# Attention projections on row halves of the TensorE array for six head pairs, and a new instruction order, in a float32 kernel of linear attention and a Fourier-mixing MLP

## The chip, the core and the metric

The kernel runs on one core of one Trainium2 chip. Its time is device time in microseconds (us), the median of three runs. The profile is that of one execution, taken by the hardware profiler; its span runs from the first to the last instruction of the core, and the execution's own time is a little longer than its span. TensorE (PE) multiplies matrices and transposes through an identity; its weight loads are a row of their own (PEld). VectorE (DVE), ScalarE (ACT) and GpSimd (POOL) do the elementwise work, SyncE (SP) issues nearly all DMAs.

## The reference

Everything is float32. Eight batches, eight heads, 576 tokens, head dimension 64, 128 random features; the model dimension is 512, the hidden one 2048.

```python
def phi(x):                                   # x = q or k, scaled by D**-0.25
    proj = np.einsum('bhsd,md->bhsm', x, omega)
    sq = np.sum(x * x, axis=-1, keepdims=True) / 2.0
    h = proj - sq
    h = h - np.max(h, axis=-1, keepdims=True)
    return np.exp(h) / np.sqrt(m)
...
kv = np.einsum('bhsm,bhsd->bhmd', k_p, v)
z = np.sum(k_p, axis=2)
num = np.einsum('bhsm,bhmd->bhsd', q_p, kv)
den = np.einsum('bhsm,bhm->bhs', q_p, z)[..., None] + 1e-06
attn = num / den                              # then (B,H,S,D) -> (B,S,H*D) = x
...
X = np.fft.fft(np.fft.fft(x, axis=1), axis=2)
u = x + np.real(X)
un = (u - mean(u)) / np.sqrt(var(u) + 1e-06)
out = u + np.maximum(un @ w_ch1, 0.0) @ w_ch2
```

The term `sq` drops out when the maximum is subtracted, so the kernel computes only `proj`.

## The kernel before

The work has two stages. In the first, the attention runs over 32 head pairs (two heads of one batch, `NP = 4` pairs a batch), three pairs at a time as three streams (`NS = 3`: pairs n, n + 3, n + 6, ... belong to one stream). After the four pairs of a batch comes its Fourier mixing (`mix`), done with matrix products against cosine and sine tables after folding; the sums go to DRAM (`us`). Between these the first 512 rows of the MLP (`plain`, four tiles of 128 rows) are computed in the ordinary way, the two weight matrices are loaded and converted (`weights`, `narrow`), and their sums for the second stage are prepared. The second stage computes the other 4096 rows in eight blocks of 512, with products split by a Strassen-like scheme (`first_of`, line 1239; `product_of`, line 1419).

A pair runs so. SyncE loads k and q (`loads`, two buffers, `NKQ = 2`) and v (`load_v`, three buffers). Of every pair there are 18 chunks of 64 columns and 128 rows; two chunks at a time are turned by TensorE (`transposed`, line 511, nine transposes in three groups, the k chunks first), and ScalarE moves them to `kqT` (line 521). The group that holds q chunks also waits for q; the last group gives the buffer back. The projections follow (`pairs_of`, line 593): for each of the nine 128-column blocks of `kqT`, whose two 64-row halves are two different chunks, four matmuls of a 64x64 tile against `om2` (64x128, twice, in the upper and lower partitions). Each works on one quarter of the array. A float32 matmul appears in the profile as two passes, a transpose as one. VectorE takes the maximum (line 537), ScalarE the exponential (line 554), which gives the features `e`. Then k features times v (line 627, on quarters) give `kv`, the q features are turned (line 511, `qeT`, line 528), and the two meet in lines 674 and 682 on column halves. VectorE or ScalarE divides (lines 691 to 703).

The order of all instructions of the first stage is fixed ahead of time by a planner in the file itself. Every piece of work is a `Step` that yields an engine, an estimated duration, the events it needs, the buffers it takes and gives, and, for TensorE, a tiling mode (`whole`, `quarters`, `halves`); the streams are generators of such steps. At each turn the planner chooses one of the waiting steps; the string `PICKS` has one character for each turn that says which, and on which of two engines where the step allows it. So the string alone fixes the sequence on each engine: the durations are used to place steps that can choose among PSUM banks and buffers. The instructions then stand in that order in each engine's queue, and each waits by semaphores for what it needs. The second stage has no such string and is planned by its durations.

TensorE's program of matmuls and weight loads is read by the core from memory as it runs (queue q8 of the profile's third part), while SyncE's loads run on the same 16 DMA engines.

Of the kernel before, what the change touches and what calls it, by code (L numbers as in the profile page):

```python
# [35 lines left out]
PE, ACT, DVE, POOL, SP, NONE = "pe", "act", "dve", "pool", "sp", "none"  # L36
# [3 lines left out]
class Clock(NamedTuple):  # L40
# [20 lines left out]


PICKS = (
    "40e0f03eafdaegebg3bdbbeefccdcccfce8affgg0hhig8ib2La887efjjgeeejjHhighifdjgijdlhhefTfkkefeifhbdfiefhi"
    "hfjgfkd9elelkjdheefdefQRLbce9h77gh7ijg8cbi877ggk7fihjmngeed87TdecedhIa7g9gg99ieeccdHcdggbhfcgfebbaci"
    "ebccebRfiedaeecf98g7fI7hh1hgg89g6gh8eecg96geaefehceaefg78hh7i9bk79jQ9ghjjf86k6ddkgjdldgiiidhfhcgfhhd"
    "eifjhf6ldinliiIlghgjibmmmILfhflkfljafLLL77lkjmehcomL9pjjjdjOa9hj6a8hhibfegbgij87ddQe9jhljiimidkhgmkj"
    "mjgiiilhkfjThfgiikj9jfmfigieiccb7ki9lll8j0k64c59kik5k86lhh7hge7h6ekie5if9ghccdfihddiifaedleeifM75fce"
    "jkd8bjicj8f8imim9fa3j8iglmn9cjfmiib8kdigce7ikiknmkmbh4cpfdbDqSZllmnFFo5nkaf9bejkllj9ak7hhg9iUhigih8T"
    "lmeIeeggkidlcm7mjdhhddbi77ibKckeiedb4ice8hb6hah8SceghihiMg5eghklfgiih9Ig7gg9b69hh9bKcbgbch54Q78higfi"  # L70
    "deeffg5ddfjcTcdigjeiedfgjhdmInmTjcgfedjhdbh67egkOa9khgkSa9hh5eghdf99bhgdegdacjgckeccgckhfhckdk9jJjij"
    "JQec9agba8cLa75i5ggih6hdUdG6j8jjTPjgg9gk57f5hdieleigIdejeihdiijkiGgibeL7875g7jgh6U8a99mmijh8jfk8kgea"
    "jf9di4gf6c5gei5ea9becjeeecghghbcjcdkfhgglfljkjh9giiackibhe5nebkkf9kJ55o4mkllQmifebek4jij557iikk9jjji"
    "mikhjkkhkiikikjlinij5JnPfjNF7efdffcc78b5kjj8lk6bae6i95W98jg3fhRefm66nfikkehhkmlcccffifhihjj6nldmiimn"
    "lmldofkhndamm48a47j4hf5khaaa8nkmm68mkj76lijknSk8iiJi9gknihne43lmccicjomaEONU76jh7mopkhjbinpijbhkkiIl"
    "5bh7jidl6klbSfihhagll50jT7eg7eikhjhh7gkhfikj0gcdcifdbiehijfmlcn2Ob5mm3k9acdc8h9g5h7eedhdgd77cbQd5gg2"
    "e9e367e78hibbMG4bbb58ccK9dLa8cfea2fecKdebecdeccefbIPbcb9hdhM6k52gbbMg5bfP7NR987ac98NPb85e8de5e6c5ec9"
    "ahagabc9dcecaeee5d8ababb9c899cKd9bedccde7fc98dgSghedggig18789bi6G45jjUi1e9gRc5863f4feL69afg3MRd8b4Eg"
    "gdc6bbe4ddeehdheimfhbifamfgccebcddhidjgjedddeT47466g4PgQ4eff1a977bb3bb833aLJ579b395I99ab9e998dbab694"
    "7c9dddgdf5hhhPfe9ead9cce7G9ed34438ge9FdHc9dcLd5ed98LcddbhheabedabddfhePdcfaafffI4daaJ9Mcce8beefd4cc2"  # L80
    "adeab27OOOM8a9K5659b0664dccdda7a2ccMccd40296cdeIP97ce8bcf6c8ddabac1aaI9d52bb9e661abec5D915G7bcd5Ed9C"
    "5bHHa9983763a3b4399F5414335aaaaE499954423225530320210"
)


# [195 lines left out]
def kernel(  # L281
# [12 lines left out]
    B, H, S, D = q.shape  # L294
# [13 lines left out]
    P = 128  # L308
# [4 lines left out]
    NV = 3  # L313
    NKQ = 2
    NE = 7


    TP = 128
# [31 lines left out]
    buffers = dict(  # L350
        kq=NKQ, turned=NS, e=NE, e1=NS, kv=NS, x0=1, x1=1, fold=1, half=1, y=1,
        bmp=2, sign=1, slab=4, u=2, unT=1, ht=NFC, ur=1, **{f"vd{i}": 1 for i in range(NV)},
# [7 lines left out]
    def got():  # L360

        return listing.got, psum_of(listing.got)
# [16 lines left out]

    def load_v(n):  # L380
        b, pr = divmod(n, NP)
        yield Step(SP, 0.63, 4.0, take=(f"vd{n % NV}",), makes=("vd", n), kb=500, bias=0.52)
        nc.sync.dma_start(
            vds[n % NV][:, :, 0:D],
            v[b, 2 * pr : 2 * pr + 2].rearrange("i (p r) d -> (i p) r d", r=R),
        )

    def loads_v():
        for n in range(B * NP):
            yield from load_v(n)  # L390
# [139 lines left out]
    def softmax(n, ts, num, b, es):  # L530

        yield Step(DVE, 0.063 + 0.267 * num, bias=-0.56)
        nmx = small.tile([P, 2, 4], F32, name="nmx", tag="nmx", bufs=4)
        pps = psum_of(b)
        nc.vector.tensor_reduce(  # L537
            nmx[:, :, 0:num],
            pps[:, :, 0 : MF * num].rearrange("p b (c m) -> p b c m", m=MF),
            axis=AX.X,  # L540
            op=ALU.max,
            negate=True,
        )
        size = "e" if num == 4 else "e1"
        for i, one in enumerate(b):
            if num == 4 or not i:
                yield Step(
                    ACT, 1.0 if num == 4 else 0.5, 0.04, take=(size,),
                    give=(one,) if num == 4 else (b,), makes=("e", n, ts[i]), bias=0.31,
                )  # L550
                e = att.tile([P, 4 if num == 4 else 2, MF], F32, name="e", tag=size, bufs=NE if num == 4 else NS)
                es[ts[i]] = e
            for c in range(num):
                nc.scalar.activation(  # L554
                    out=e[:, c + (i if num == 1 else 0), :],
                    in_=pps[:, i, MF * c : MF * c + MF],
                    func=AF.Exp,
                    bias=nmx[:, i, c : c + 1],
                )

    def attn(n):
# [13 lines left out]
        )  # L575
        es = {}

        def pairs_of(js, *ts):


            yield Step(
                PE,
                0.23 * len(js),
                mode="quarters",
                after=(("kqT", n, js[-1] // 4 * 4), "om2"),
                take=("duo",),
                give=("turned",) if js[-1] == R - 1 else (),
            )
            b, pps = got()
            for m, j in enumerate(js):  # L590
                for c, i in ((0, 0), (1, 1), (0, 1), (1, 0)):
                    rows, cols = slice(D * c, D * c + D), slice(D * i, D * i + D)
                    nc.tensor.matmul(  # L593
                        pps[cols, c, MF * m : MF * m + MF],
                        lhsT=kqT[rows, j, cols],
                        rhs=om2[rows, :],
                    )
            yield Fork(softmax(n, ts, len(js), b, es))


        yield from pairs_of(range(0, 4), 0, 1)
        yield from pairs_of(range(4, 5), 2)
        yield from pairs_of(range(5, R), 3, 4)

        def place(c):
# [4 lines left out]
        def feature(c):  # L610
# [7 lines left out]
            mode="quarters",  # L618
            after=tuple(("e", n, t) for t in range(3)) + (("vd", n),),
            take=("duo",),  # L620
# [3 lines left out]
        for r in range(R):  # L624
            for i, h in ((0, 0), (1, 1), (0, 1), (1, 0)):
                rows, cols = slice(D * i, D * i + D), slice(D * h, D * h + D)
# [9 lines left out]
        def keep():  # L636
# [24 lines left out]
            mode="halves",  # L661
            after=(("kv", n), ("qeT", n, 0), ("qeT", n, 1), ("qeT", n, 5)),
            take=("duo",),
# [526 lines left out]
    def pairs(start):  # L1190
        for n in range(start, B * NP, NS):
            yield from attn(n)
# [364 lines left out]
```

## Time and profile before

| what | value |
|---|---|
| median of 3 runs | 1185.65 us (1182.2 to 1187.07) |
| profiled execution: its own time | 1187.5 us |
| its span | 1185.6 us, 31878 instructions |
| TensorE busy | 1165.1 us (98%), 12765 passes |
| weight loads | 1044.6 us (88%) |
| VectorE, ScalarE, GpSimd busy | 697.8, 470.1, 417.6 us |
| first stage, to the first line-1239 product | 428.44 us |
| TensorE, ScalarE, VectorE busy in it | 412.77, 300.22, 315.95 us |
| mean granted clock | 0.996 |

The share of the span of the chain that ended last is 92% TensorE. TensorE's busy time includes ends that are modelled, so the price of a group of instructions is read from its start to the start of the next group, less the idle time that the timeline puts before that next group. In a timeline line the columns are the start and length in us, the engine and line, the operation, what is written from what, the tile of the array (rows*columns), the shape, the number of passes, and in brackets the idle time before the group and what ended it.

### The profile page before, as it was taken

What the parts mean: (1) busy time and instruction counts of PE and PEld (TensorE: products, weight loads), DVE (VectorE), ACT (ScalarE), POOL (GpSimd) and SP (SyncE); (2) the same over time, 40 slices, a digit from 0 to 9 for tenths busy, and PEclk for the clock granted to TensorE, in tenths of its full rate; (3) what the DMA queues carried; (4) which work ended last, traced back from release to release, by engine and by line L of the source; (5) the groups of instructions that cost most, each with busy time, mean ns of one, the idle gap of its engine ahead of it and who ended that gap; (6) DMA issues with size and microseconds to landing.
All of it is one profiled execution on the core that took longest, in us unless ns stands there. A gap on an engine that the chain in (4) does not pass through costs nothing.

```text
span 1185.6 us, 31878 instructions
## 1 busy us (share of the span) xinstructions
PE 1165.1 (98%) x12765; PEld 1044.6 (88%) x12765; DVE 697.8 (59%) x1488; ACT 470.1 (40%) x1597; POOL 417.6 (35%) x496
## 2 busy tenths in 40 slices
PE   7999999999999999999999999999999999999998
PEld 6888888779877868998998998999999899899898
DVE  4898899886656542762572582473374276266255
ACT  5988888868654212222222222222222222222211
POOL 2353544444344314314304314323422431431421
PEclk8999999999999999999999999999999999999999
DMA  8566856656654161761682482384195085177155
GB/s 250 165 186 182 252 172 194 186 164 193 188 194 157 45 212 50 261 211 63 205 264 74 154 290 100 99 294 149 48 303 192 10 290 191 54 240 240 63 165 192
DMA packets 144708, 205.71 MB, mean 174 GB/s; under 512 B 49072, under 2 KB 58544, under 8 KB 144560
## 3 DMA queue, kind: packets, MB, share of 16 engines
q1 hardware_dynamic: 144064, 203.41, 54.1%
q8 instruction: 101, 1.65, 0.6%
q14 instruction: 47, 0.39, 0.1%
q10 hardware_dynamic: 496, 0.26, 0.1%
HBM read 171.90 MB, written 35.91 MB: 175 GB/s over the span
## 4 chain that ended last, share of the span: by engine, by line
PE 92%; ACT 2%; DVE 2%; DMA 2%; issue 1%; SPq 1%; POOL 0%; DVEq 0%; ACTq 0%
PE banks L1239 33%; PE banks L1419 30%; PE banks L1055 5%; PE banks L1032 5%; PE banks L511 5%; PE banks L593 4%; PE banks L627 3%; PE banks L674 2%; PE banks L972 2%; PE banks L836 1%; ACT e L554 1%; PE banks L786 1%; PE banks L796 1%; DMA kq<-in_q_dram 1%; PE banks L847 1%
## 5 line engine op out<-in xcount | busy, mean ns | idle before, releaser
L1225 DVE CUSTOM_DVE_ANT_0 hid<-banks,s 128x256 f32<-128x256 f32 x192 | 79.6, 422 | 255.4 <-PE banks L1239 250.5
L1419 PE MATMUL banks<-wl,sums 128*128 128x128 f32 x1792 | 217.5, 275 | 0.0
L1419 PEld LDWEIGHTS banks<-wl,sums 128*128 128x128 f32 x1792 | 208.9, 192 | 0.5
L1253 ACT ACTIVATE s<-banks 128x256 f32<-128x256 f32 x192 | 73.6, 383 | 261.7 <-PE banks L1239 261.7
L554 ACT ACTIVATE e<-banks,nmx 128x128 f32<-128x128 f32 x576 | 164.7, 437 | 16.3 <-DVE nmx L537 15.7
L1239 PE MATMUL banks<-unT,w 128*128 128x256 f32 x704 | 167.5, 379 | 0.0
L1239 PEld LDWEIGHTS banks<-unT,w 128*128 128x128 f32 x704 | 132.7, 190 | 17.9 <-issue 0.5
L1394 ACT ACTIVATE s<-banks 128x128 f32<-128x128 f32 x168 | 46.5, 277 | 242.6 <-PE banks L1419 196.0
L1239 PE MATMUL banks<-tt,w1s 128*128 128x256 f32 x512 | 126.2, 379 | 0.0
L1306 POOL TENSOR_TENSOR hs<-hid 128x256 f32<-128x256 f32 x64 | 46.4, 725 | 202.9 <-DVE hid L1225 178.6
L537 DVE TENSOR_REDUCE nmx<-banks 128x8 f32<-128x1024 f32 (+1 forms) x96 | 89.0, 952 | 34.1 <-PE banks L593 31.8
L1239 PEld LDWEIGHTS banks<-tt,w1s 128*128 128x128 f32 x512 | 97.2, 190 | 13.3
L1399 DVE TENSOR_TENSOR part<-banks,s 128x128 f32<-128x128 f32 x168 | 48.8, 291 | 89.0 <-PE banks L1419 88.7
L1419 PE MATMUL banks<-wl,hid 128*128 128x128 f32 x768 | 97.6, 275 | 0.0
L1419 PEld LDWEIGHTS banks<-wl,hid 128*128 128x128 f32 x768 | 93.5, 192 | 1.2
L1306 POOL TENSOR_TENSOR hs<-hid,hs 128x256 f32<-128x256 f32 x64 | 46.5, 727 | 120.4 <-issue 95.4
L593 PE MATMUL banks<-om,kqT 64*64 64x128 f32 x2304 | 78.4, 276 | 2.4 <-issue 0.9
L1239 PE MATMUL banks<-unT,w1s 128*128 128x256 f32 x320 | 80.7, 379 | 0.0
L966 POOL TENSOR_TENSOR rstd<-rstd,mhalf 128x1 f32<-128x1 f32 x36 | 24.1, 668 | 146.1 <-DVE rstd L964 145.1
L1419 PE MATMUL banks<-wl,hs 128*128 128x128 f32 x576 | 74.9, 275 | 0.4 <-DVE part L1399 0.4
L593 PEld LDWEIGHTS banks<-om,kqT 64*64 64x64 f32 x2304 | 63.9, 134 | 12.2 <-issue 4.3
L1419 PEld LDWEIGHTS banks<-wl,hs 128*128 128x128 f32 x576 | 70.0, 192 | 0.9 <-DVE part L1399 0.6
(129 smaller groups left out, 1957.0 us busy)
## 6 DMA issues: line engine op xcount, KB each, us to landing
wl<-w2l SPq DMA_DIRECT2D x392, 256.0 KB, 3.6
raw<-in_moe_w_ch_dram SPq DMA_DIRECT2D x32, 512.0 KB, 5.2
kq<-in_k_dram SPq DMA_DIRECT2D x32, 288.0 KB, 4.5
kq<-in_q_dram SPq DMA_DIRECT2D x32, 288.0 KB, 5.1
vd<-in_v_dram SPq DMA_DIRECT2D x32, 288.0 KB, 4.6
u<-us SPq DMA_DIRECT2D x36, 256.0 KB, 4.0
ur<-us SPq DMA_DIRECT2D x36, 256.0 KB, 3.8
out_dram<-ur SPq DMA_DIRECT2D x34, 256.0 KB, 2.4
```

The lines of the kernel that those rows point to most:

```text
L511: nc.tensor.transpose(ps[:, (j - j0) * 128 : (j - j0 + 1) * 128], src(j), ident[:])
L537: nc.vector.tensor_reduce(nmx[:, :, 0:num], pps[:, :, 0 : MF * num].rearrange("p b (c m) -> p b c m", m=MF), axis=AX.X, op=ALU.max, negate ...
L554: nc.scalar.activation(out=e[:, c + (i if num == 1 else 0), :], in_=pps[:, i, MF * c : MF * c + MF], func=AF.Exp, bias=nmx[:, i, c : c + 1],)
L593: nc.tensor.matmul(pps[cols, c, MF * m : MF * m + MF], lhsT=kqT[rows, j, cols], rhs=om2[rows, :],)
L1032: nc.tensor.matmul(hp[:, 0:TP], lhsT=w1[:, dc, 128 * fc : 128 * fc + 128], rhs=unTs[key][:, dc, :], start=(dc == 0), stop=(dc == NDC - 1),)
L1055: nc.tensor.matmul(yp[:, 0:DM], lhsT=hs[fc][:, 128 * i : 128 * i + 128], rhs=w2[:, fc, :], start=(fc == 0), stop=(fc == NFC - 1),)
L1225: nc.vector._custom_dve(TENSOR_ADD_SAT, out=o, in0=ps, in1=sb, s0=FMAX, s1=0.0)
L1239: nc.tensor.matmul(ps[:, 0:HT], lhsT=left(dc), rhs=right(dc), start=start and dc == 0, stop=(dc == D2 - 1), skip_group_check=True,)
L1253: nc.scalar.activation(out=s[:], in_=ps[:, 0:HT], func=AF.Copy)
L1306: nc.gpsimd.tensor_tensor(out=o, in0=l, in1=r, op=op)
L1399: nc.vector.tensor_tensor(out=part[:, t, 128 * m : 128 * m + 128], in0=ps[:, 0:128], in1=saved[with_][:], op=ALU.add,)
L1419: nc.tensor.matmul(ps[:, 0:128], lhsT=left[:, f], rhs=wls[j, i, n][:, f], start=start and f == 0, stop=(f == 3), skip_group_check=True,)
```

## The change

It has three parts. For the first six pairs (`n < NWIDE`), `pairs_of` issues two matmuls a block in place of four: each takes a 64x128 tile of `kqT` on one half of the array's rows, and writes all 128 output partitions. The planner's step gets a tiling mode `rows` and a duration of 0.25 a block in place of 0.23. All other pairs keep the quarters. The planner's duration for issuing a v load goes from 0.63 to 1.15. And `PICKS` is replaced: the first characters are alike, most of the rest differs, so the order of the first stage changes on every engine. The work itself is otherwise the same.

```diff
 PICKS = (
-    "40e0f03eafdaegebg3bdbbeefccdcccfce8affgg0hhig8ib2La887efjjgeeejjHhighifdjgijdlhhefTfkkefeifhbdfiefhi"
...
+    "40e0f03eafdaegebg3bdcbeefccdcccfc8aggh0gjihij8c2M99887eejgffjgHeefgikedlekddkidfffffkkheeeegjiigOKdh"
...
+    NWIDE = 6
...
-        yield Step(SP, 0.63, 4.0, take=(f"vd{n % NV}",), makes=("vd", n), kb=500, bias=0.52)
+        yield Step(SP, 1.15, 4.0, take=(f"vd{n % NV}",), makes=("vd", n), kb=500, bias=0.52)
...
+        wide = n < NWIDE
+
         def pairs_of(js, *ts):
-
             yield Step(
                 PE,
-                0.23 * len(js),
-                mode="quarters",
+                (0.25 if wide else 0.23) * len(js),
+                mode="rows" if wide else "quarters",
                 after=(("kqT", n, js[-1] // 4 * 4), "om2"),
                 take=("duo",),
                 give=("turned",) if js[-1] == R - 1 else (),
             )
             b, pps = got()
             for m, j in enumerate(js):
-                for c, i in ((0, 0), (1, 1), (0, 1), (1, 0)):
-                    rows, cols = slice(D * c, D * c + D), slice(D * i, D * i + D)
+                for c, i in ((0, 0), (1, 0)) if wide else ((0, 0), (1, 1), (0, 1), (1, 0)):
+                    rows, cols = slice(D * c, D * c + D), slice(D * i, P if wide else D * i + D)
                     nc.tensor.matmul(
                         pps[cols, c, MF * m : MF * m + MF],
                         lhsT=kqT[rows, j, cols],
                         rhs=om2[rows, :],
                     )
```

The order on SyncE at the start, which the prediction speaks of, by what is loaded (numbers are issues since the first; w is a piece of a weight matrix, one comma-separated entry is one step):

```
issue   before                                      after
1-14    k q v v k q k w q w k q cs cs               the same
15-20   sn sn w v w v                               w sn sn w v k
21-26   v k cd cd q k                               cd cd v w q k
27-33   w w w q k sd sd                             w v w q sd sd v
```

On TensorE the two orders run as follows after the first pair's k v product (lines of before; passes in brackets):

```
before: 511 k(4) 593(40) 511 e(9) 511 k(5) 627(72) 674(32) 682(8) 511 e(1) 593(32) ...
after:  593(4) 511 e(1) 593(16) 511 k(8) 511 e(8) 511 k(1) 627(72) 674(32) 682(8) 593(16) ...
```

More of the change, by code (lines that the diff above doesn't have):

```diff
@@ L63 @@
 PICKS = (
-    "40e0f03eafdaegebg3bdbbeefccdcccfce8affgg0hhig8ib2La887efjjgeeejjHhighifdjgijdlhhefTfkkefeifhbdfiefhi"
[L65 to L82, printed above, removed]
+    "40e0f03eafdaegebg3bdcbeefccdcccfc8aggh0gjihij8c2M99887eejgffjgHeefgikedlekddkidfffffkkheeeegjiigOKdh"
+    "ddfdgel8dlglkjfhdfefgQeQgLd7787eihfigegbbb88i8f7jhikigjmfdddfdifeiihHdcccffeddccddIHcggafbgaddadbhbf"
@@ new lines @@
+    "cdebRfiddiaeecf877gbe7ii1ihhae7hige7k8hgdfcehghfcGefga8hg7ghhabk89jQ9ghjjf86k6ddkgjdldhigidhcigfIegg"
+    "cdifjhf6kijchljmjblhjjobnHLknjkhkQmgdkjakLMLm87kjjcfed9nbkia9kkif6jaj8iedhheckgj8b7dSckle7eichgjjckl"
+    "miikffhgjjkfefiTflkkiglhghmhjec7b99jjk0jh64d66k9hk97mkhhhhhMef7ehig69dchdg6iaedleldkbcgdbmfmh57bhikg"
+    "g5jg8djibj7a7imim8f3kbjhlmn7dgcm8lknig7fkfmmc6mnollbjipi6ofecbDoecWhlijlghmnlmeccXljnbiohjibikilgnLm"
+    "kiFp6Fgdfjk8i7l9cebb9kahiaagHk7Rfeia46abjedbRfhgaehfa8NKeed5a5f9cceijfhhahccgg6aidgg4SHf98hh47bhigfi"
@@ new lines @@
+    "eeeffe5ehddehfhadiePffdlhfkTjU9hgeihcdfi889cg9h9fhkkiefihSbahh5bghgcbgfhhafhfebajmiefggkgcj9gjiiJJPb"
+    "b9fdbac86j65kjhkk7h78eUj87Uk96kklkfTQkfg9hl6H5jeoipefffghhGfkeeihOjhig8n78l5fam8Wfbb8nllVcha5ghmfj9l"
+    "jmdb6j4hc6ad5hejhbd9deffPediffgghedjkicliiiijkhjhkad9iglbge5ngbkkf9kJ644olkoQifebek4ji6ii57iil9jjjhi"
+    "lklhnkjlhkkjkilinijcYn59FmeLMgddijcc78maldj58cb7ja5Wa9jkhTfkjf3e8mPd6liilgkjdcmjffgnf7dfflmlghkknjkn"
+    "efghPojEkimjfeYanl4nnmf566m44nnjSe9b68l6ljkjljbkkdUihihkb3h5ilfilTdh6ckj6l6le5iemHLIT5j48jbGibkjjj7h"
@@ new lines @@
+    "jahihf4jhflkkamjj9jjm40llbifgkiijahjiifjj0hhjjee5cdjdidfihejT7c37kkk4id98abghah6if7ccecOfcd8db6ii2a9"
+    "gbdfcdfaae53af78ccG7d8Kb9M78cfaggg8RcdgcdgbbK2gcNbacdfNcbfgO642577M9fa9Pdd8bbfdMa9de5OLN5ee75cbbf6aa"
+    "5becbbdeada9fbcd9bfbb5bgaehaQccddg9dabgb8db7kk2LI143gfg556a87f4f46bfQgegcfecQ8fa4eccMRefSf69dfeg7aLE"
+    "9d7ffec6fe3fdchhgiccbQ4daij6ck8ad8jdgegfhc98eh9dgeagbfE6e6d5144b544994c96689ab4466a8485c79e7779e5a89"
+    "6ece65fd5defP8ff33e7cbh7bJIEE9b4gaaga8I3d898Hfe8OcLN49cd9b6N8f88efdeFN9bahghfghe7IebOgeehbac92feLe2c"
@@ L83 @@
+    "dce979ccK9aKJ9b879a0Bd1a54babbb1b4278aKaa7c9Nc9c7aac8c9f6M076198cM65604a87abac83Fbac7499bbG1063b7aKa"
+    "Jc9768971bHC628bcc6b5a6c3647C877550777662230242132110"
 )
```

## The prediction

> **What bounds the kernel now.** I read the windows first: they split the span where the second half of the MLP begins.
>
> ```profile
> core 0: us, PE busy (x) PEld busy (x) DVE busy (x) ACT busy (x) POOL busy (x), PEclk, DMA share, GB/s
> 0.00:428.44 428.44, 412.77 (x7726) 341.58 (x7727) 315.95 (x686) 300.22 (x1090) 179.26 (x187) 0.99 0.60 179
> 428.44:1185.60 757.16, 752.31 (x5041) 703.00 (x5039) 381.81 (x802) 169.85 (x507) 238.29 (x309) 1.00 0.52 170
> ```
>
> From 428.44 us on, TensorE's instruction order is the same in both kernels (the first difference, counted from the end, lies before the line-1239 products), so those 757.16 us stay. What can change lies in the first 428.44 us, and TensorE is the bound there too: it is idle for only 428.44 - 412.77 = 15.67 us. TensorE's waits say what those are.
>
> ```profile
> engine line waited for: us in total, times, longest us
> PE banks L674 <- issue: 4.6, 1, 4.6
> PE banks L511 <- DMA kq<-in_q_dram: 2.0, 2, 1.6
> PE banks L511 <- ACT e L554: 1.9, 2, 1.3
> PE banks L511 <- DMA kq<-in_k_dram: 1.5, 1, 1.5
> PE banks L593 <- issue: 0.9, 1, 0.9
> ```
>
> "Issue" means that nothing the profile shows was waited for. The timeline of TensorE shows where:
>
> ```profile
> 14.22 0.65 PE L593 MATMUL banks<-om,kqT 64*64 64x128 f32 x10
> 15.78 1.10 PE L593 MATMUL banks<-om,kqT 64*64 64x128 f32 x30 [0.91 <-issue]
> 16.81 1.20 PE L511 MATMUL banks<-ident,e 128*128 128x128 f32 x9
> 17.85 0.71 PE L511 MATMUL banks<-ident,kq 128*128 128x128 f32 x5
> 18.49 1.28 PE L627 MATMUL banks<-vd,e 64*64 64x65 f32 x72
> 19.70 0.56 PE L674 MATMUL banks<-kv,qeT 128*64 128x65 f32 x11
> 24.84 1.36 PE L674 MATMUL banks<-kv,qeT 128*64 128x65 f32 x21 [4.57 <-issue]
> ```
>
> Both waits cut a group of equal matmuls in two. Between them lie 30 + 9 + 5 + 72 + 11 = 127 passes, each with its weight load: 254 instructions, [...]. Before the first wait lie 221 passes. So the program's text came late, while the loads had the DMA engines (third column from the end is the clock, then the DMA share):
>
> ```profile
> 20.00:22.00 2.00, 0.26 (x9) 0.13 (x6) 0.40 (x2) 2.00 (x8) 1.46 (x2) 1.00 1.17 319
> 22.00:24.00 2.00, 0.00 (x0) 0.00 (x0) 0.00 (x0) 0.20 (x1) 1.33 (x1) 0.76 1.23 265
> 24.00:26.00 2.00, 1.16 (x23) 1.16 (x24) 0.00 (x0) 0.00 (x0) 0.00 (x0) 0.50 0.63 119
> 26.00:28.00 2.00, 2.00 (x33) 1.65 (x33) 1.19 (x3) 0.89 (x3) 0.00 (x0) 0.50 0.89 255
> ```
>
> The reader sees the clock fall to 0.50 after the wait, and ScalarE run dry as well, so the lost time is not made up elsewhere.
>
> [...] TensorE's instruction queue moved 101 packets, 1.65 MB. [...]
>
> **The change part by part.** Prices come from TensorE's timeline, start to next start:
>
> ```profile
> 43.47 1.10 PE L593 MATMUL banks<-om,kqT 64*64 64x128 f32 x32
> 44.50 0.77 PE L511 MATMUL banks<-ident,e 128*128 128x128 f32 x5
> ...
> 46.07 1.32 PE L593 MATMUL banks<-om,kqT 64*64 64x128 f32 x40
> 47.33 0.33 PE L511 MATMUL banks<-ident,kq 128*128 128x128 f32 x1
> ...
> 63.42 0.81 PE L796 MATMUL banks<-cs_sb,fold 64*128 64x320 f32 x4
> 64.17 1.09 PE L511 MATMUL banks<-ident,e 128*128 128x128 f32 x8
> ```
>
> Four chunks of projections take 1.03 us to the next kind, five take 1.26: 0.23 us a chunk on quarters and 0.11 us for the change of tiling mode (a fit over all groups of the stage gives 0.232 and 0.107).
>
> 1. *Row halves.* 6 pairs x 9 chunks = 54 chunks go from 4 matmuls to 2, so from 8 passes to 4. The only row of this kind is L796: four passes of 320 columns in 0.75 us, less one mode change 0.64, so 0.32 for two side by side. A whole-array pass takes 0.115 us at 128 columns and 0.147 at 160, so near 0.28 at 320: the two do overlap, at 0.04 over a pass. A chunk is two such couples of 128 columns: from 2 x 0.115 = 0.23 to 2 x 0.155 = 0.31. I take 0.25: 54 x 0.02 = +1.0 us (bounds 0 and +4.3).
>
> 2. *Text.* 54 x 8 = 432 instructions go, 1.7 blocks. Priced by the fit, the blocks that start at passes 94, 221, 348 and 475 hold 3.9, 4.3, 5.9 and 3.0 us of TensorE work before; in the changed order they hold 5.2, 5.9, 4.6 and 5.3, and the next one 7.6. Before, the second block came 3.9 + 0.91 = 4.8 us after the first began, which 5.2 covers: -0.91. The third came 24.84 - 15.78 = 9.1 us after; if that stays, 9.1 - 5.9 = 3.2 us of 4.57 remain. I expect less: the same first fourteen DMAs are issued, but the two v loads that kept SyncE's queue busy for 3.45 us from 18.45 no longer come back to back; k, a table and one v load stand there. I take 1.0 left (bounds 0 and 3.2). Later blocks ran through in as little as 3.5 and 3.9 us without a wait before, so the usual fetch is that fast.
>
> 3. *Clock.* From 24.84 to 29.78 us TensorE did work worth 2.70 us by the fit (21 + 8 + 1 + 32 + 4 passes and three mode changes), in 4.94: 2.24 lost. [...]: -2.24.
>
> 4. *Order of the k and q loads.* Two buffers hold k and q, so a pair's load starts when the transposes of the pair two before are done. In TensorE work between them, pair 16's q half has 6.4 us before and waited 1.60 us at 124.75; in the new order it has 8.8. Pair 25 has 4.95 and waited 0.40 at 222.15; now 5.7. Both waits should go: -2.0. Pairs 10 and 13 keep 6.5 and 5.8, as the ones that did not wait for DMA. SyncE's sequence there is nearly the same, so nothing new stands before these loads. The first k wait (1.54 us at 9.03) follows the same DMAs and stays.
>
> 5. *Other reordering.* The new TensorE order has 253 mode changes in this stage against 232: 21 x 0.107 = +2.25 us. 1.7 us of the extra TensorE work of parts 1 and 5 lies before the eighth pair ends, where TensorE waits for ScalarE now (0.57 + 0.19 + 0.42 + 0.35 + 0.16 = 1.69 us between 36 and 60). ScalarE is 99% busy at 40 to 60 us, so it can hide some: I take -0.5. Without that cover, 0. The 1.29 us wait at 89.38 for ScalarE keeps its neighbours in the order: 0. The changed price of the v load (1.15 for 0.63) is no instruction; it acts through the order alone. At the stage's end the last norm transposes stand before 8 matmuls of L1055 (16 passes x 0.43 = 6.9 us) instead of before 12 + 16 passes of other work; two evictions and four adds of line 1100 (2.5 us) have to fit, and do: 0.
>
> Sum: -0.91 - 4.57 + 1.0 - 2.24 - 2.0 + 1.0 + 2.25 - 0.5 = -5.97 us. The profiled execution took 1187.5 us (span 1185.6 and 1.9 around it), so 1181.5 in its terms; it stood 1.85 above the median of 1185.65, which becomes 1179.7. ScalarE is late next: with the gap gone it runs through from 10 to 60 us.
>
> **The rivals.** *Given back.* The text comes half as late and the new order waits for ScalarE or a load in new places, for 3 to 4 us: the 4.3 us of small waits now are spread over many engines, and a searched order shifts all of them. The gain is 2 to 3 us, 1183. For it: the orders on VectorE, ScalarE and GpSimd all differ from the start; against: the pairs finish at nearly the same amounts of TensorE work (0.5 to 3 us apart through most of the stage). *Fetch stays slow.* A k load, a table and more weights now follow without a pause where SyncE before issued nothing from 26.4 to 32.85 us. If each of four blocks takes 9.1 us to come, the waits are 9.1 less 5.9, 4.6, 5.3 and 7.6: 13.0 us, and two clock drops of 2.2 more. Then -7.7 - 2.0 + 3.25 + 17.4 = +10.9: 1196.6, slower. It decides from about 7.4 us a fetch, where the first three waits eat the rest of the gain (3 x 7.4 - 15.8 = 6.4). For it: the one fetch seen in the burst took 9.1; against: at 38 to 48 us, DMA share 0.76 to 0.98, none was late. *Row halves in series.* Four passes of 0.115 are 0.46 a chunk: 54 x 0.21 = 11.3 more than I take, 1191; L796 speaks against it. *More.* The small waits for ScalarE go too, and the fetch is never late: 1.0 + 4.3 us more, 1174.5.
>
> **How the numbers follow.** 0.5% (5.9 us) is about what a measurement of this kernel can tell from no change. The forecast, 4 to 9 us off, has 0.52, and 0.28 of that is past 5.9; "more" 0.12; "given back" 0.20; slow fetch 0.11, serial halves and the like 0.05, of which 0.01 stays inside 0.5%. Faster 0.28 + 0.12 = 0.40; same 0.24 + 0.20 + 0.01 = 0.45; slower 0.15. Range 1174 to 1191: it holds the forecast, "given back" and nearly all of "more" and leaves out the slow fetch. The likeliest case's own range is 1176 to 1182.
>
> **What would show it.** Right: no issue wait over 2 us before 60 us, clock 1.00 in the windows from 22 to 30; projections of 0.25 us a chunk in a 64*128 tile; no wait for q near 120 or 220 us; the first line-1239 product near 422.5 us, and 757 us after it. Wrong: a wait cutting a group in two at every 127th pass, a clock of 0.50 elsewhere, or L554 and L521 in front of TensorE's idle time where they are not now.

## The result, and the profile after

| | before | after |
|---|---|---|
| median | 1186.66 us (20 runs, 1182.20 to 1191.15) | 1182.66 us (20 runs, 1180.12 to 1185.49) |
| profiled execution, its span | 1187.5, 1185.6 us | 1183.56, 1181.8 us |

The ratio of the times is 0.9967, with a 95% interval of 0.9956 to 0.9978: 4.0 us less, 0.33%. That is inside the 0.5% that the prediction took for no change, but twenty runs of each tell it from none. The profiled executions differ by 3.9 us, so they can stand for the medians. In the code after, most of the lines spoken of stand one or two lower (593 is 595, 511 is 512, 627 is 629, 674 is 676, 912 is 914, 1239 is 1241).

The windows of the changed kernel, split at its first line-1241 product (busy us of each engine, then clock, DMA share, GB/s):

```profile
0.00:424.44 424.44, 413.60 (x7510) 340.52 (x7511) 316.61 (x681) 298.72 (x1088) 186.49 (x194) 1.00 0.62 183
424.44:1181.80 757.36, 752.26 (x5041) 703.09 (x5039) 381.93 (x802) 169.85 (x507) 238.26 (x309) 1.00 0.52 169
```

Before, that product began at 428.28 us (the prediction's split, 428.44, lies 0.16 behind its start), so that the second stage took 757.32 us and takes 757.36 now. All of the change is in the first stage, 3.84 us. TensorE is idle for 424.44 - 413.60 = 10.84 us of it, 15.67 before, and 0.8 us busier. The new `PICKS` also moves work between engines: over the whole execution VectorE has five instructions fewer, ScalarE two, and GpSimd seven more (503 for 496). TensorE's waits, by what ended them:

```profile
engine line waited for: us in total, times, longest us
PE banks L512 <- DMA kq<-in_q_dram: 2.8, 2, 2.5
PE banks L512 <- DMA kq<-in_k_dram: 2.2, 1, 2.2
...
PE banks L595 <- issue: 0.8, 1, 0.8
PE banks L676 <- issue: 0.4, 2, 0.2
```

The 4.6 and 0.9 us of "issue" have become 1.2 in three pieces, but the waits for loads of k and q, 3.5 us before, are now 5.0. TensorE's timeline of the place where the 4.57 us stood:

```profile
24.67 0.82 PE L595 MATMUL banks<-om,kqT 64*128 64x128 f32 x9
26.26 0.71 PE L595 MATMUL banks<-om,kqT 64*128 64x128 f32 x7 [0.78 <-issue]
26.90 0.77 PE L512 MATMUL banks<-ident,kq 128*128 128x128 f32 x5
27.60 1.16 PE L595 MATMUL banks<-om,kqT 64*128 64x128 f32 x16
28.69 1.28 PE L629 MATMUL banks<-vd,e 64*64 64x65 f32 x72
29.90 0.49 PE L595 MATMUL banks<-om,kqT 64*128 64x128 f32 x4
30.46 0.91 PE L676 MATMUL banks<-kv,qeT 128*64 128x65 f32 x23
31.59 0.51 PE L676 MATMUL banks<-kv,qeT 128*64 128x65 f32 x9 [0.22 <-issue]
```

Projections stand in a 64*128 tile, 16 passes for four blocks. A group is again cut in two by a wait for nothing that the profile shows, and from one cut to the next lie 7 + 5 + 16 + 72 + 4 + 23 = 127 passes, as before, but holding more work. The instruction queue of the two pages' third part, before and then after (packets, MB, share of the 16 DMA engines' span):

```profile
q8 instruction: 101, 1.65, 0.6%
```
```profile
q8 instruction: 99, 1.62, 0.6%
```

TensorE's 12765 passes with their weight loads are 253 instructions for each of the 101 packets, and 12549 are 254 for each of the 99: the length from one cut to the next, and 432 instructions less are 2 packets less. So a packet is read here as one block of TensorE's text, and such a wait as a block that came late; no view shows when a single packet landed. The windows there:

```profile
22.00:24.00 2.00, 2.00 (x25) 1.67 (x21) 1.97 (x4) 1.59 (x8) 0.51 (x1) 1.00 1.22 291
24.00:26.00 2.00, 1.49 (x17) 1.16 (x14) 1.35 (x4) 2.00 (x8) 2.00 (x2) 1.00 1.16 225
26.00:28.00 2.00, 1.74 (x18) 1.45 (x19) 0.92 (x1) 1.34 (x7) 0.72 (x1) 1.00 0.98 290
```

The DMA share is as high as before (1.16 and 1.22), but the clock stays at 1.00 where it was 0.76 and 0.50. By the same group of 30 passes of L595 (55.39 us; 59.80 before) the changed kernel is 4.4 us ahead; from there to the second stage it loses 0.57. TensorE's timeline shows a place of the loss:

```profile
85.03 0.63 PE L512 MATMUL banks<-ident,kq 128*128 128x128 f32 x4 [2.54 <-DMA kq<-in_q_dram]
```

It waits 2.54 us for the tenth pair's q, which the kernel before did not. SyncE's waits (total, times, longest) and then its timeline lead to what stood ahead of that load:

```profile
SPq L914 <- POOL x L900: 38.0, 6, 15.9
```
```profile
71.97 1.22 SPq L914 DMA_DIRECT2D us<-x  x2
73.30 0.53 SPq L376 DMA_DIRECT2D kq<-in_k_dram  x1
73.92 1.98 SPq L469 DMA_DIRECT2D raw<-in_moe_w_ch_dram  x1
75.99 1.94 SPq L384 DMA_DIRECT2D vd<-in_v_dram  x2
77.98 2.26 SPq L379 DMA_DIRECT2D kq<-in_q_dram  x1
```

Before, the tenth pair's k, the store and q stood so:

```profile
68.80 0.33 SPq L375 DMA_DIRECT2D kq<-in_k_dram  x1
...
77.08 1.90 SPq L912 DMA_DIRECT2D us<-x  x2
...
79.71 0.71 SPq L378 DMA_DIRECT2D kq<-in_q_dram  x1
```

At 71.97 us SyncE comes out of a wait of 15.9 us for GpSimd's `x` (line 900), which a store of the first mixing result needs. Behind it in the queue stand the tenth pair's k, a weight piece, two v loads, and only then q, issued at 77.98. Before, the store stood between k and q. With the 4.4 us that the changed kernel is ahead, 79.71 would be 75.3; its q is 2.7 us later than that. The store itself comes 5.1 us earlier than before. What is new is how much was put behind it: from the store to q pass 6.0 us, where it was 2.6.

### The profile page after: what moved, and what is told of

It reads as the page before. It is cut to its first block, busy times and chain, and to the rows that moved or that the text cites. A ratio compares the mean times of both kernels' runs of the same rounds, so it can differ in the third digit from the quotient of the medians.

```text
span 1181.8 us, 31441 instructions
## 1 busy us (share of the span) xinstructions
PE 1165.9 (99%) x12549; PEld 1043.6 (88%) x12549; DVE 698.5 (59%) x1483; ACT 468.6 (40%) x1595; POOL 424.7 (36%) x503
## 4 chain that ended last, share of the span: by engine, by line
PE 90%; ACT 4%; DVE 2%; DMA 2%; issue 1%; POOL 0%; SPq 0%; DVEq 0%; POOLq 0%; ACTq 0%
PE banks L1241 33%; PE banks L1421 30%; PE banks L1057 5%; PE banks L1034 5%; PE banks L512 4%; PE banks L595 3%; ACT e L555 3%; PE banks L676 2%; PE banks L629 2%; PE banks L974 2%; PE banks L838 1%; PE banks L788 1%; DMA kq<-in_q_dram 1%; PE banks L798 1%; ACT kqT L522 1%
## 5 line engine op out<-in xcount | busy, mean ns | idle before, releaser
L595 PE MATMUL banks<-om,kqT 64*64 64x128 f32 (+1 forms) x2088 | 79.8, 275 | 2.2 <-ACT kv L645 0.8
L595 PEld LDWEIGHTS banks<-om,kqT 64*64 64x64 f32 (+1 forms) x2088 | 64.6, 138 | 13.3 <-issue 6.6
```

The lines of the kernel that those rows point to most:

```text
L595: nc.tensor.matmul(pps[cols, c, MF * m : MF * m + MF], lhsT=kqT[rows, j, cols], rhs=om2[rows, :],)
```

## The experiments

Eleven runs: nine new kernels, one of them twice, and the changed kernel again. `PICKS` is adapted in each new kernel so that only what is named differs: where loads move, SyncE's order; where row halves come or go, the projections on TensorE. The planner's choice of PSUM banks is fixed in all of them, apart from the repeat of the changed kernel, to that of the kernel they start from, which adds lines to the file (595 is 607, 629 is 641, 676 is 688, 914 is 926).

| kernel | median us | ratio to before, 95% interval | runs |
|---|---|---|---|
| quarters in the new order | 1188.37 | 1.0013 (1.0002 to 1.0025) | 22 |
| row halves in the old order | 1189.48 | 1.0024 (1.0012 to 1.0035) | 22 |
| row halves for three pairs, old order | 1187.00 | 1.0002 (0.9988 to 1.0017) | 14 |
| new load order at the start, else before | 1187.90 | 1.0006 (0.9995 to 1.0018) | 14 |
| before, tables late | 1186.23 | 0.9993 (0.9976 to 1.0009) | 14 |
| after, tables late | 1183.26 | 0.9969 (0.9958 to 0.9981) | 22 |
| after, tenth pair's loads ahead of the store | 1182.30 | 0.9968 (0.9957 to 0.9979) | 22 |
| after, second pair's k and q first | 1181.32 | 0.9953 (0.9939 to 0.9967) | 22 |
| the same again | 1181.98 | 0.9956 (0.9939 to 0.9972) | 13 |
| after, both moves | 1180.55 | 0.9946 (0.9927 to 0.9966) | 8 |
| after, again | 1182.06 | 0.9960 (0.9943 to 0.9976) | 11 |

### One part of the change at a time

The new order with the projections on quarters:

```diff
-    NWIDE = 6
+    NWIDE = 0
```

> The changed kernel with the quarters back for the first six pairs (36 matmuls a pair in place of 18), every engine's order otherwise as in the changed kernel. Theory text: the row halves matter because they thin the program. With quarters the first fetched blocks hold 3.7, 4.5, 6.0, 2.8 us of TensorE work in place of 5.2, 5.9, 4.6, 5.3, so an issue wait of 2.5 to 4.5 us comes back between 18 and 28 us, with the clock at 0.50 after it: +4 to +6 us on the changed kernel, near 1187. Theory order: the new order of loads had removed the wait; then no issue wait over 1 us, and 1 us less than the changed kernel for cheaper projections, 1181.5.

And the old order, old durations, with row halves for the first six pairs (the diff of `pairs_of` alone):

> The kernel before with row halves for the first six pairs and nothing else changed, its own order on every engine. Theory text: the blocks hold 5.1, 5.6, 5.0, 5.2 us instead of 3.9, 4.3, 5.9, 3.0; the issue waits fall from 5.5 us to 1 to 3.5, the clock stays at 1.00, row halves cost 1 us: 1181 to 1184. Theory order: waits as before, 1187.5.

Neither part gains alone: both are slower than before, by 0.13% and 0.24%. In the first the waits for text are back, in the order that had 1.2 us of them, as its timeline shows:

```profile
15.80 1.09 PE L607 MATMUL banks<-om,kqT 64*64 64x128 f32 x27 [0.87 <-issue]
23.75 1.45 PE L688 MATMUL banks<-kv,qeT 128*64 128x65 f32 x21 [2.53 <-issue]
35.66 0.51 PE L688 MATMUL banks<-kv,qeT 128*64 128x65 f32 x9 [1.02 <-issue]
41.59 0.45 PE L641 MATMUL banks<-vd,e 64*64 64x65 f32 x12 [0.91 <-issue]
```

That is 5.3 us in the first 60 (5.5 before, there in two waits), and the clock fell too: 0.50 from 24 to 26 and 0.83 from 26 to 28 us. The second stage begins at 430.06 us, 5.6 after that of the changed kernel. So the row halves, not the order, take these waits away.

In the second kernel the front is as good as hoped (one wait for text of 0.94, clock 1.00, the group that stood at 58.12 before at 54.15), and the 4 us are lost again later: its second stage begins at 430.96, 2.7 later than before. The largest loss, in its timeline (line 696 is 682 of before) and its windows:

```profile
135.88 0.33 PE L696 MATMUL banks<-kv,qeT 128*64 128x65 f32 x2 [2.59 <-issue]
```
```profile
122.00:132.00 10.00, 9.83 (x296) 8.49 (x289) 9.36 (x15) 9.83 (x39) 7.02 (x6) 1.00 0.90 295
132.00:134.00 2.00, 1.29 (x38) 1.15 (x38) 1.61 (x3) 2.00 (x10) 0.74 (x1) 1.00 0.52 179
134.00:136.00 2.00, 0.12 (x2) 0.12 (x2) 0.00 (x0) 0.87 (x4) 0.78 (x1) 1.00 0.69 144
136.00:138.00 2.00, 2.00 (x11) 1.62 (x11) 1.50 (x4) 0.00 (x0) 0.00 (x0) 0.63 0.92 294
138.00:140.00 2.00, 2.00 (x73) 1.98 (x72) 1.86 (x4) 1.87 (x7) 0.00 (x0) 0.51 0.43 96
```

It is the pattern of 24 us over again, with a DMA share of 0.90 over the ten us ahead, a block of text late, and the clock at 0.63 and 0.51 after it, where the kernel before ran through. Two waits for q of 1.46 and 1.19 us at 120.56 and 154.09 come with it. Every block border after the first six pairs has moved against the loads.

To see whether the borders do it, the old order got row halves for three pairs only, so that the borders move half as far:

```diff
-    NWIDE = 6
+    NWIDE = 3
```

> The kernel before, its own order, with row halves for the first three pairs only. The first blocks hold 5.1, 5.6, 4.1, 5.0 us, so the early issue waits are 1 to 2.5 us in sum and the clock stays up. The text is 108 passes shorter than before, not 216, so all later block borders lie elsewhere. Theory borders: the 2.59 us issue wait that row halves for six pairs brought at 136 us (and the clock drop after it) is a matter of where a border falls against a burst; here it is under 1 us: 1183 to 1186. Theory pace: with the front faster, the later loads and text are late anyway; an issue wait of 2 us or more comes near 135 us again: 1188 to 1190.

At 135.50 us there is 0.27 left of the 2.59, but 1.89 stand at 189.60 in its place and 2.17 for a q at 222.39. Its waits for ScalarE grew most, by 3.8 us over before in the first stage. The time, 1187.00, is that of before and lies in neither of the ranges expected. That the place of the wait moves with the borders is seen; which border will meet a burst could not be told ahead.

### The order of the loads, and what they do to the text

The kernel before, with SyncE's first steps in the changed kernel's sequence (w is a piece of a weight matrix, cs, sn, cd, sd are the tables of two issues each, numbers are pairs):

```diff
 k0 q0 v0 v1 k1 q1 k2 w q2 w k3 q3 cs
-sn w v2 w v3 v4 k4 cd q4 k5 w w w q5 k6 sd v5 v6 q6
+w sn w v2 k4 cd v3 w q4 k5 w v4 w q5 sd v5 k6 w v6 q6
```

> The kernel before with only SyncE's issues 13 to 36 put in the sequence that the changed kernel has (the two v loads apart, a weight load and k ahead of them). Theory order: the second block's fetch takes 7.2 us as in the changed kernel, not 9.1, so the wait of 4.57 falls to about 2.7 and the clock drop mostly goes: 1182 to 1184. Theory text: the fetch is as late as before, 4 to 5 us of wait and the clock drop stay: 1186 to 1188.

The wait at 24.52 us is 4.28, and the clock 0.84 and 0.50 from 24 to 28. The order of these loads alone did nothing for the text, and the prediction's thought that a k load and a table in place of two v loads would speed up the fetch has no support.

The opposite test takes loads out of the burst: the four tables (0.90 MB) are loaded only after the sixth pair's q, in each of the two kernels. In the kernel before:

```diff
-cs sn w v2 w v3 v4 k4 cd q4 k5 w w w q5 k6 sd
+w v2 w v3 v4 k4 q4 k5 w w w q5 cs sn cd k6 sd
```

> The kernel before with the four cosine and sine tables (0.83 MB, of which 0.64 were asked for at 12 to 15 us) loaded after the sixth pair's q instead; nothing but SyncE's order differs, quarters throughout. Theory contention: the text comes late because it shares the DMA engines with the burst of loads; 0.64 MB at about 0.29 MB a us is 2.2 us less in front of it, so the wait of 4.57 us falls to about 2.4 and part of the clock drop goes: 1183 to 1185. Theory fixed latency: a text block takes 9 us there whatever else is loaded; the wait stays at 4 to 5 us: 1186 to 1188.

> The changed kernel with the four tables loaded after the sixth pair's q. Theory contention: the three issue waits (0.78, 0.22, 0.20 us) go: 1181.5. If the fetch does not depend on the load, they stay: 1182.7. A bound: in neither case more than 1.2 us of gain from text; if it is later than 1184, the tables or the k loads behind them have become late near 60 us.

In the kernel before, TensorE's timeline and a window:

```profile
22.39 0.85 PE L686 MATMUL banks<-kv,qeT 128*64 128x65 f32 x21 [2.01 <-issue]
```

```profile
20.00:22.00 2.00, 0.37 (x11) 0.24 (x9) 0.98 (x3) 2.00 (x9) 1.10 (x1) 1.00 0.57 124
```

4.57 became 2.01 us for the same 21 passes, with the same program text. The DMA share from 20 to 22 us was 0.57 for 1.17. So most of this wait, 2.56 us of it, came with the loads that were taken out of the burst. In the changed kernel the 1.20 us of text waits went to nothing before 60 us. Yet both kernels took the time of those they were made from. In the first, new waits for text of 0.43 and 1.29 us at 126.81 and 272.78 and for loads of 0.78 and 0.86 at 174.46 and 322.15 stand against the gain. In the second these are waits for q of 1.80 at 40.30 and 1.79 at 84.12, the latter with 32 projection passes of 1.99 us behind it, which took 1.10 at 88.53, and for text of 0.72 and 0.57 at 95.23 and 100.08. That these waits come from the tables is not shown. The second kernel's profiled execution, 1185.95 us, also lies 2.7 above its median.

### The waits for loads that stayed or came

The tenth pair's k and q ahead of the store, and the eleventh pair's q ahead of the next (us and uh are the stores, of two issues each):

```diff
-us k9 w v9 v10 q9 k10 uh q10
+k9 q9 us w v9 v10 k10 q10 uh
```

> The changed kernel with four moves on SyncE's queue only: the k and q loads of the tenth pair (counted from 1) go ahead of the store of the first mixing result, which waits 15.9 us there, and the eleventh pair's q ahead of the copy to uh. Theory queue: the 2.54 us wait for q at 85 us and the 0.28 at 87.7 come from that store standing ahead of the loads; they go, 1180. Rival: another wait for ScalarE takes their place, as 1.29 us did there in the kernel before: 1181.5. Rival contention: the load is late because the DMA engines are full, and nothing is gained: 1182.7.

SyncE's timeline shows k and q issued early, and the store behind them:

```profile
64.60 0.33 SPq L388 DMA_DIRECT2D kq<-in_k_dram  x1
64.98 0.42 SPq L391 DMA_DIRECT2D kq<-in_q_dram  x1
72.10 1.23 SPq L926 DMA_DIRECT2D us<-x  x2
```

The wait of 2.54 us is gone, as it should be if the store caused it; the group that followed it came 1.6 us earlier (95.25 for 96.81). But the second stage began at 425.83 us, 1.4 later than in the changed kernel, after waits for q of 0.64 at 138.20 and 1.24 at 173.53 and with 2.5 us of waits for text instead of 1.2. This profiled execution took 1184.96 us, 2.7 above the median of its runs, so that part of the loss can be scatter. The median is the same as the changed kernel's within 0.4 us: no gain can be told.

The second pair's k and q ahead of the two v loads:

```diff
-k0 q0 v0 v1 k1 q1 k2 w q2 w
+k0 q0 k1 q1 v0 v1 k2 w q2 w
```

> The changed kernel with the second pair's k and q loads ahead of the first two v loads on SyncE's queue; nothing else differs. Theory path: the 2.16 us wait for k at 9.24 us goes and all that follows comes 1.5 to 2 us earlier: 1181. Theory cover: ScalarE is busy without a gap from 10 us and sets the pace; the gain up to 20 us is under 0.7 us, or v is late instead: 1182 to 1183.

TensorE's timeline there:

```profile
5.71 1.42 PE L607 MATMUL banks<-om,kqT 64*128 64x128 f32 x20
7.05 0.65 PE L524 MATMUL banks<-ident,kq 128*128 128x128 f32 x4
```

The transposes of k begin at 7.05 instead of 9.24 us with no wait, and at 52.88 the same group stands 2.5 us ahead of the changed kernel. The median was 1.3 us less. To see how sure that is, and whether the two moves add, three kernels were timed beside each other.

> The changed kernel itself, timed beside the two that follow, so that they are compared with it under the same conditions. Expected: ratio to the kernel before 0.9967 within 0.001, that is about 4 us less, and in its profile again a wait of TensorE for the tenth pair's q of 1 to 3 us near 85 us and one for the second pair's k of about 2 us near 9 us. If these two waits come out far from that, a single profile's wait for a load is not a property of the kernel.

> The changed kernel with the second pair's k and q ahead of the first two v loads, a second time. If the 2.16 us wait for k is really on the path and its removal is kept to the end, the ratio is 0.995 to 0.996 and 1 to 2 us below the changed kernel of the same batch. If the gain measured the first time was scatter, it is within 0.5 us of the changed kernel.

> The changed kernel with both moves on SyncE: the second pair's k and q ahead of the first two v loads, and the tenth pair's k and q ahead of the store of the first mixing result, the eleventh pair's q ahead of the store after it. If removed waits add up, the two give the 1.3 us of the first move alone plus up to 1.5 us of the second: ratio 0.993 to 0.995. If what is gained at the second place is given back later, as it was when that move was made alone, the ratio is that of the first move alone, 0.995 to 0.996, with new waits for q or for instructions after 95 us.

The changed kernel's time came again (1182.06), but not its wait. In TensorE's timeline the first eight transposes of the tenth pair, four of k and four that need q, run through, and the eleventh pair's q, which had cost 0.28 us, is waited for:

```profile
81.24 1.14 PE L512 MATMUL banks<-ident,kq 128*128 128x128 f32 x8
...
85.34 0.77 PE L512 MATMUL banks<-ident,kq 128*128 128x128 f32 x5 [1.20 <-DMA kq<-in_q_dram]
```

The second stage began at 421.93 instead of 424.44 us. So a wait of 2.5 us for a load in one profile can be absent from the next. The store's part shows over all profiles: where it stands ahead of the loads (this kernel twice, the second pair's loads first twice, the tables late) the two q cost 0.75 to 2.82 us together, and in both kernels with the loads ahead nothing. The first move alone was 0.1 us from the changed kernel this time; over all runs of both, 35 and 31, the means differ by 0.56 us (95%: 1.42 less to 0.36 more), which is not told from nothing. The two moves together were 1.4 us below the changed kernel beside them in the mean (0.3 to 2.5), and 1.6 below all of its runs (0.7 to 2.5). Their ratio, 0.9946, lies where added gains were expected, but its interval covers both expectations. The two places of the new waits for q in the kernel with the tenth pair's loads ahead cost 0.20 us here, so those waits do not follow from that move. This is the fastest version, 5.6 us below before. In the first stage its TensorE waits for 6.3 us in all, of which loads are 0.4:

```profile
PE banks L524 <- DMA kq<-in_q_dram: 0.4, 2, 0.2
```

## Why the prediction came out as it did

It forecast 6.0 us less; 4.0 were measured, inside its range and nearer to its rival "given back". The waits of the first stage, as the timeline brackets them, and the other terms, set against its sum (profiled executions, us):

| term | forecast | measured | from |
|---|---|---|---|
| text (part 2) | -4.48 | -5.20 | issue waits 6.40 before, 1.20 after |
| clock (part 3) | -2.24 | -2.24 | 1.00 in every window from 20 to 28 us; the size is the prediction's |
| k and q loads (part 4) | -2.00 | +1.44 | waits for loads 3.54, 4.98 |
| waits for ScalarE (part 5) | -0.50 | -0.75 | 3.77, 3.02 |
| waits for VectorE | 0 | -0.07 | 1.42, 1.35 |
| row halves, mode changes | +3.25 | +2.98 | what remains |
| sum | -5.97 | -3.84 | start of the second stage, 428.28 and 424.44 |

The remainder is the least sure: the same account (waits, clock, and 0.107 us for each of 246 and 237 mode changes) leaves 1.4 us unplaced for the quarters in the new order, and 1.9 for the row halves in the old one.

1. *Row halves* (0.25 a block): right. Sixteen passes in the 64*128 tile run from 27.60 to 28.69, 1.09 us, less a mode change of 0.107: 0.246 a block, where the rival of row halves in series had 0.46: the two halves overlap, and that rival is dead.

2. *Text* (1.0 us left): right in size, in part by luck: 1.20 stayed; beyond the sum, the small text waits after 60 us went too (0.9 before). The quarters in the new order, with 5.3 us of waits for text in the first 60, show that it is the thinner text that does it. One reason given for a small rest, the order of the loads, fell with the experiment on it; the third block did come 7.2 us after the second began (19.06, by counting 127 passes back, to 26.26) and not 9.1, but what shortened this is not shown. "Fetch stays slow" did not come: the next blocks were 0.22 and 0.20 late.

3. *Clock*: right, and the quarters in the new order lost it again. But it was not as safe as the forecast took it, which counted the whole 2.24 as won while its bounds for the text left waits of up to 3.2 us: after waits of 2.53 and 2.01 us in two of the experiments the clock stood at 0.50 from 24 to 26 us.

4. *Order of the k and q loads*: here the prediction failed. The waits of 1.60 and 0.40 us at 124.75 and 222.15 did go (the loads that ended them are, counted from the first, the fourteenth and the twenty-third q; the prediction calls the pairs 16 and 25). But "SyncE's sequence there is nearly the same, so nothing new stands before these loads" was wrong for the tenth pair: a store that waited 15.9 us for GpSimd stood ahead of its k, a weight piece and a second v load as well as its q, and q came 2.54 us late, its successor 0.28. The first k wait stayed, at 2.16 us for 1.54; with the same loads ahead of it, it was 1.86, 1.22 and 1.05 in three other profiles, so this growth is scatter. The term came out 3.44 us above its forecast, the other terms together 1.31 below theirs, and that is the 2.13 by which the sum was off. In the second profile of the changed kernel the loads cost 3.64 us, so that some of this term is scatter, but even there nothing of the forecast 2.0 appears. In that profile the second stage begins 6.35 us before that of the kernel before, near the forecast; the medians of the two timings, 4.0 and 4.1 us less, point to the smaller gain. How much of the missing 2 us is this term stays open.

5. *Other reordering* (21 mode changes, ScalarE's cover): the changed kernel's timeline has 21 mode changes more than that of before, as forecast, and their price, with that of the row halves, fits the remainder.

What "given back" said is what happened in the first profile, for about 2 us: a new wait, for a load, in a new place, after a front that was 4.4 us ahead. The experiments also say why an order had to be searched. With row halves in the old order the same 4 us were won at the front, and 6.65 lost after it. That most of it was lost in waits for text and for loads, and in the lower clock after one of them (0.63 and 0.51), is seen in the trace; why each single one came where it did stays open, and so does why removed waits did not shorten the median when the tables were put off or the tenth pair's loads moved ahead.

## What to carry to other kernels

An "issue" wait that cut a group of equal matmuls, 127 passes after the one before it in both kernels, was read as the program's text coming late: it shrank with the loads beside it (4.57 to 2.01 us). Fewer, wider matmuls, half the passes for a block of projections, made the text last longer, and in the new order they were worth it at 0.25 us a block for 0.23 (1182.66 us against 1188.37). Such a change moves all later blocks against the loads, so time it together with a new order of the work, never by the front alone. SyncE sent the tenth pair's k at 73.30 us behind a store that waited 15.9, and at 64.60 where it stood ahead of that store. So look at what a store waits for before putting a load behind it, and time the kernel before believing in a single removed wait: here two of them together gave 1.4 us, and each alone nothing that can be told.

## What the runs showed of the hardware

Counted from the start of the block before it (no view shows when a block is asked for), a block of TensorE's text came within 3.9 (the prediction's fit) + 0.9 = 4.8 us in one place of the kernel before, with a DMA share of 0.96 to 1.01 in the windows from 10 to 16 us, and in the next only after 9.1, with 0.94 to 1.23 from 16 to 24; with the tables out of the burst this was 22.39 - 15.81 = 6.6. In the kernel before, the waits for text were 6.4 of 428 us, and after the longest, 4.57, the clock was 0.50 from 24 to 28 us.

The clock fell after some of the waits and not after others. A wait of 2.53 us (quarters in the new order) and one of 2.01 (before, tables late) were each followed by 0.50 from 24 to 26 us, while waits of up to 1.12 near that time (second pair's k and q first, again, at 24.88) left it at 1.00. After 1.79 us (after, tables late, at 84.12) 32 projection passes took 1.99 us, for 1.10 at 88.53. But after the changed kernel's 2.54 us at 85.03 the clock was 1.00 from 84 to 90 us, and after the 2.17 at 222.39 with row halves for three pairs eight passes of 160 columns took 1.25 us, as they did at 182.22. So in these runs the length of a single wait does not decide it.

Two v loads in a row held SyncE's queue for 2.43 us at the start of the changed kernel (1.63 us on) and for 1.52 when two pairs' k and q went ahead of them, against 0.42 for one q.
